# Four pieces of work moved inside the attention steps of a fused attention and Fourier-mix kernel

## The chip, the cores and the metric

One core of a Trainium2 chip runs the whole program in one launch. The metric is the device time of a launch in microseconds (us), lower is better. The engines of a core are TensorE (PE for its matmuls, PEld for its weight loads), VectorE (DVE), ScalarE (ACT), GpSimd (POOL) and SyncE (SP). In this program SP computes nothing: nearly all DMAs are issued from its queue, in the order in which the program wrote them, and an issue that has to wait for data holds up every issue behind it.

## What is computed

For 8 batches of 8 heads, with 576 rows and a head size of 64, an attention with a threshold; its result, laid out as 576 x 512 per batch, goes through a two-dimensional Fourier transform of which the real part is added, a layer norm, and a channel MLP of 512 to 2048 to 512. All is in fp32.

```python
scores = scale * np.matmul(q, k.transpose(0, 1, 3, 2))
thresh = np.max(scores, axis=-1, keepdims=True) - tau
scores = np.where(scores >= thresh, scores, -1000000000.0)
attn = np.exp(scores - max); attn = attn / (sum + 1e-09)
x = (attn @ v)                       # (B,H,S,D) -> (B, S, H*D)
u = x + np.real(np.fft.fft(np.fft.fft(x, axis=1), axis=2))
un = (u - mean) / np.sqrt(var + 1e-06)
out = u + np.maximum(un @ w_ch1, 0.0) @ w_ch2
```

## The kernel before

**Steps.** Two heads make a pair `n`, four pairs make a batch, and a pair takes five steps `t` = 0 to 4 of 128 query rows each (the fifth has the last 64 rows of both heads). So there are 160 steps `i`, 20 in a batch; below, s is `i` modulo 20, so that s = 0 to 4 belong to a batch's first pair, 5 to 9 to its second, and so on. The pairs of a batch are taken in the order 1, 3, 0, 2 of the heads' pairs; the first two of these have v stored with its columns reversed, and need their rows 0 and 64 exchanged afterwards.

**A step of the main loop (lines 1764 to 1837, batches 2 to 7).** TensorE makes the scores (`scores`). DVE takes the row maxima (line 518), ACT the exponentials (524), DVE compares and sums (539), and ACT scales by the sums (552). Around this the loop calls `fill` three times. A `fill` issues a little of the MLP of earlier rows: as much as a running budget says, so it is the same number of pieces in every run. The call order in a step is: scores; the values of an earlier pair; `softmax_first`; `fetch`; `fill(True)`; `softmax_second`; `blocks`; row exchanges that stand in `swaps`; `weights_in_parts`; `fill`; `softmax_third`; `prep_pair` and the like; `fill`; loads of v, q or k.

**The MLP** of 512 rows (`two_level`) runs a first layer of 28 blocks of 8 matmuls each (line 1288, about 10 steps), and then a second of 49 blocks of 4 matmuls (line 1437, the other 10 steps). Its weights come by DMA into a ring of five places (`ensure`, lines 1155 to 1165), four places ahead. A block of the first layer with m = 7 adds onto the bank that the block with m = 6 left, so it can start only when DVE has added that bank to `hs` (line 1225). Between them lies one other block.

**Two ways to transpose the softmax's result** for the product with v. In the second layer TensorE transposes and ACT copies. In the first layer (`phase[0] == 1`) a step goes by DMA (`decide`): `blocks` lets DVE sort its tile into blocks of 32 x 32 (line 601, into the one room `et_room`) and SP write it to memory (602), one step after the step itself; `fetch` reads it back in four DMAs two steps after (611). `et_room` can be written again when the DMA of 602 has landed. From batch 3 on these are, in each batch, the steps s = 6, 7, 8 (second pair), 10 to 13 (third pair) and 15 (fourth pair), 40 in all.

**The product with v** (`values_in_parts`) has a first part of 256 query columns, and a second of 320. By default the first part is issued at t = 3 and the second at t = 1 of the next pair. Where the pair went by DMA, the first part is issued at t = 0 of the next pair, and the second at t = 1 of the next pair behind `fill(True)` (`late_values`). So these second parts are at s = 11 and s = 16.

**Row exchange.** `swap_rows` copies two rows out by two DMAs (line 759) and back crosswise by two more (763). For a batch's first pair it is called in `fold_rows`: copy of the tile on POOL (line 779), both pairs of DMAs, and then the fold itself (792 onward). `fold_more` takes the next piece of it: at t > 2 and from some blocks of the MLP. The first piece falls to the last `fill` of s = 6.

**prep_pair** (403 to 416) lets DVE transpose k and q of the next pair (lines 410, 411, 413) at t = 3. **v_of** (578) lets POOL make the reversed v, called in `weights_in_parts` at t = 1. **load_raw** loads q at the end of t = 0 and k at the end of t = 1; **load_v** loads v at the end of t = 2.

Of the kernel before, what the change touches and what calls it, by code (L numbers as in the profile page):

```python
# [47 lines left out]
def kernel(  # L48
# [500 lines left out]
    def softmax_third(i):  # L549
        nh, e, den = steps[i]  # L550
        for j in range(nh):
            nc.scalar.activation(  # L552
                out=e[:, S * j : S * (j + 1)], in_=e[:, S * j : S * (j + 1)], func=ACT.Copy,
                scale=den[:, j : j + 1],
            )
        if nh == 1:
            nc.scalar.copy(e[:, S : S + 64], e[:, 512:S])
        steps[i] = (e, None)
# [4 lines left out]
    def in_blocks(n):  # L563

        return n >= 3 * NPAIR
# [5 lines left out]
    def decide(i):  # L571

        n, t = divmod(i, NT)
        by_dma[i] = i < B * NPAIR * NT and in_blocks(n) and t < 4 and (
            phase[0] == 1 or t == 2 and by_dma[i - 1]
        )

    def v_of(n):

        src = heads[n][2]  # L580
        if PAIRS[n % NPAIR] % 2 == 0:
            return src
        vt = sb.tile([128, 10, D], FP32, tag="vr", bufs=1, name="v_rev")
        nc.gpsimd.tensor_copy(vt[:, :, 0:1], src[:, :, 0:1])
        last = src[:, :, D - 1 : D]
        down = bass.AP(
            tensor=last.tensor, offset=last.offset,
            ap=[list(last.ap[0]), list(last.ap[1]), [-1, D - 1]],
        )
        nc.gpsimd.tensor_copy(vt[:, :, 1:D], down)  # L590
        return vt
# [3 lines left out]
    def blocks(i):  # L595

        if not by_dma[i]:
            return
        e = steps.pop(i)[0]
        out_ = et_room.rearrange("p (b c q) -> p c b q", b=4, c=NC9)  # L600
        nc.vector.transpose(out_, e[:, 0 : 2 * S])
        nc.sync.dma_start(out=scratch[i % 3][:, :], in_=et_room)

    def fetch(i):

# [16 lines left out]
    def weights_in_parts(i):  # L622

        n, t = divmod(i, NT)
        if in_blocks(n) and t == 0:
            heads[n] = (*heads[n][0:2], v_of(n), None, None)
        if by_dma.get(i):
            return
        e, rec = steps.pop(i)
        if in_blocks(n) and t < 4:  # L630
            to = by_block[:, first_block(t) : first_block(t) + 4]
            pe = ps.tile([128, 4, 128], FP32, tag="mm", bufs=4, name="pe")
            nc.tensor.transpose(pe[:, 0, :], e[:, 512:640], ident[:, :])
            nc.scalar.copy(to[:, :, 4, :], pe[:, 0, :].rearrange("p (a q) -> p a q", q=32))  # L634
            for j in range(2):
                pw = ps.tile([128, 4, 128], FP32, tag="mm", bufs=4, name="pw")
                if j == 1:
                    yield
                for c in range(4):
                    c0 = (S + D) * j + 128 * c  # L640
                    nc.tensor.transpose(pw[:, c, :], e[:, c0 : c0 + 128], ident[:, :])  # L641
                nc.scalar.copy(
                    to[:, :, 5 * j : 5 * j + 4, :],
                    pw[:, :, :].rearrange("p c (a q) -> p a c q", q=32),
                )
            return
        if in_blocks(n):
            pe = ps.tile([128, 4, 128], FP32, tag="mm", bufs=4, name="pe")
            nc.tensor.transpose(pe[:, 0, :], e[:, 512:640], ident[:, :])
            for j in range(2):  # L650
                hp = slice(64 * j, 64 * j + 64)
                nc.scalar.copy(
                    by_block[hp, 2:4, 4, :],
                    pe[hp, 0, hp].rearrange("p (a q) -> p a q", q=32),
                )
            pw = ps.tile([128, 4, 128], FP32, tag="mm", bufs=4, name="pw")
            for c in range(4):
                nc.tensor.transpose(pw[:, c, :], e[:, 128 * c : 128 * c + 128], ident[:, :])
            for j in range(2):
                for a in range(2):  # L660
                    nc.scalar.copy(
                        by_block[:, 2 + a, 5 * j : 5 * j + 4, :],
                        pw[:, :, 64 * j + 32 * a : 64 * j + 32 * a + 32],
                    )
            return
        if t in (0, 2):

            e_t, ends = early_e_t, early_ends  # L670
            vt = v_of(n) if t == 0 else heads[n][2]
            heads[n] = (*heads[n][0:2], vt, e_t, ends)
        e_t, ends = heads[n][3:5]
        q0 = 128 * (t - (0 if t < 2 else 2))
        pe = ps.tile([128, 4, 128], FP32, tag="mm", bufs=4, name="pe")
        nc.tensor.transpose(pe[:, 0, :], e[:, 512:640], ident[:, :])
        kept = 1
        if rec is not None:
            nc.tensor.transpose(pe[:, 1, :], rec, ident[:, :])
            kept = 2  # L680
        if t < 4:
            nc.scalar.copy(ends[:, 0:kept, q0 : q0 + 128], pe[:, 0:kept, :])
        else:
            for j in range(2):
                hp = slice(64 * j, 64 * j + 64)
                nc.scalar.copy(ends[hp, 0:kept, q0 : q0 + 64], pe[hp, 0:kept, hp])
        qs = slice(q0, q0 + (128 if t < 4 else 64))
        for j in range(2 if t < 4 else 1):
            pw = ps.tile([128, 4, 128], FP32, tag="mm", bufs=4, name="pw")
            if j == 1:  # L690
                yield
            for c in range(4):
                c0 = (S + D) * j + 128 * c
                nc.tensor.transpose(pw[:, c, :], e[:, c0 : c0 + 128], ident[:, :])  # L694
            if t < 4:
                nc.scalar.copy(e_t[:, 4 * j : 4 * j + 4, qs], pw[:, :, :])
            else:
                nc.scalar.copy(
                    e_t[:, :, qs].rearrange("p (j c) q -> p j c q", j=2),
                    pw[:, :, :].rearrange("p c (j q) -> p j c q", j=2),  # L700
                )
# [50 lines left out]
    def swap_rows(n, later=False):  # L752
        b, p = n // NPAIR, PAIRS[n % NPAIR]
        x = xs[b][p]
        if p % 2:

            swap = sb.tile([2, S], FP32, tag="half", bufs=1, name="swap")
            for j in range(2):
                nc.sync.dma_start(out=swap[j : j + 1, :], in_=x[64 * j : 64 * j + 1, :])

            def back():
                for j in range(2):
                    nc.sync.dma_start(out=x[64 * j : 64 * j + 1, :], in_=swap[1 - j : 2 - j, :])

            if late and later:
                swaps.append(back)
            else:
                back()

# [4 lines left out]
    def fold_rows(n):  # L774
        b, p = n // NPAIR, PAIRS[n % NPAIR]
        if late and n % NPAIR == 0:
            assert not mixes
            x = sb.tile([128, S], FP32, tag=f"x{p}", bufs=1, name=f"x{p}")
            nc.gpsimd.tensor_copy(x[:, :], xs[b][p][:, :])
            xs[b][p] = x  # L780
            swap_rows(n)
            yield
        x = xs[b][p]

        half = sb.tile([128, 2, HALF], FP32, tag="half", bufs=1, name="half")
# [874 lines left out]
    def fold_more():  # L1660
        if folds and next(folds[0], True):
            folds.pop(0)
# [101 lines left out]
    for i in range(2 * per_batch, total + 3):  # L1764
# [3 lines left out]
        values = iter(())  # L1768
        if i < total:
            scores(i)  # L1770
        late_values = None
        if t == 3 and i < total and not by_dma.get(i - 2):
            values = values_in_parts(n, 0)
        elif t == 0 and by_dma.get(i - 4):
            values = values_in_parts(n - 1, 0)
        elif t == 1 and n > 0:
            while folds:
                fold_more()
            values = values_in_parts(n - 1, 1)
            if by_dma.get(i - 3):  # L1780
                values, late_values = iter(()), values
        next(values, None)
        if i < total:
            softmax_first(i)
# [7 lines left out]
                pass  # L1792
            start_batch(i // per_batch - 1)
        fill(True)
        for _ in late_values or ():
            pass
        if i < total:
            softmax_second(i)
        while held:
# [4 lines left out]
            swaps.pop(0)()  # L1804
        if mixes:
            mix(1)
        if t == 1:
            if n % NPAIR:
                folds.append(fold_rows(n - 1))
            else:  # L1810
                last_fold = fold_rows(n - 1)
                next(last_fold)
        weights = weights_in_parts(i - 1) if i <= total else iter(())
# [6 lines left out]
        next(weights, None)  # L1820
        if i < total:
            softmax_third(i)
            if t == 1:
                prep_ends(n)
            if t == 2 and n + 1 < B * NPAIR:
                scale_q(n + 1)
            if t == 3 and n + 1 < B * NPAIR:
                prep_pair(n + 1)
        if wanted:
            wanted.pop().factors()  # L1830
        if i % per_batch == 1:
            next(last_fold)
        fill()
        if t == 2 and n + 1 < B * NPAIR:
            load_v(n + 1)
        if t < 2 and n + 1 < B * NPAIR and len(loaded.get(n + 1, ())) == t:
# [51 lines left out]
```

## Time and profile before

| what | value |
|---|---|
| median of 3 runs | 1634.24 us (1628.0 to 1637.57) |
| profiled execution, its own time | 1636.11 us |
| its span, first to last instruction | 1634.0 us |
| busy: PE, DVE, ACT, POOL | 93%, 69%, 55%, 50% |
| granted TensorE clock, mean | 0.973 |
| DMA engines, by SP's queue | 60.6% of the span |
| DVE transposes of line 601 | 40, 1366 ns each |
| DVE transposes of lines 410, 411, 413 | 32 each, 761, 242 and 778 ns |
| DMAs of line 602: issue to landing | 40, median 4.1 us |
| DMAs of line 611: issue to landing | 160, median 3.9 us |
| DMAs of 759 and 763: issue to landing | 32 each, 1.8 and 1.7 us |

A line of the waits names who waited, for whom, then microseconds in total, times, and the longest. A line of the timeline gives start, duration, engine, line, operation and the tiles written and read; in brackets is the engine's idle time before it and what ended it. A line of the windows gives a stretch's length, the busy time of each engine, the granted TensorE clock, and the share of the DMA engines.

### The profile page before, as it was taken

What the parts mean: (1) busy time and instruction counts of PE and PEld (TensorE: products, weight loads), DVE (VectorE), ACT (ScalarE), POOL (GpSimd) and SP (SyncE); (2) the same over time, 40 slices, a digit from 0 to 9 for tenths busy, and PEclk for the clock granted to TensorE, in tenths of its full rate; (3) what the DMA queues carried; (4) which work ended last, traced back from release to release, by engine and by line L of the source; (5) the groups of instructions that cost most, each with busy time, mean ns of one, the idle gap of its engine ahead of it and who ended that gap; (6) DMA issues with size and microseconds to landing.
All of it is one profiled execution on the core that took longest, in us unless ns stands there. A gap on an engine that the chain in (4) does not pass through costs nothing.

```text
span 1634.0 us, 27080 instructions
## 1 busy us (share of the span) xinstructions
PE 1523.9 (93%) x9410; PEld 1166.9 (71%) x9410; DVE 1130.0 (69%) x2137; ACT 904.9 (55%) x1913; POOL 813.3 (50%) x1002
## 2 busy tenths in 40 slices
PE   8998989999999989998999899998999899999997
PEld 4555545556787867876787677776787678889987
DVE  7997786846769567766677577856677666636537
ACT  5775565545666556655666566665566566233231
POOL 6784663034454623536253724553264625547646
PEclk9999999999999999999999999999999999999998
DMA  7423221645945389737975588628974696556755
GB/s 159 125 56 113 74 74 36 190 144 177 285 149 165 94 253 261 203 97 203 248 203 143 141 252 244 187 79 230 255 205 127 178 264 203 186 160 230 238 188 191
DMA packets 296253, 286.26 MB, mean 175 GB/s; under 512 B 202643, under 2 KB 241045, under 8 KB 295222
## 3 DMA queue, kind: packets, MB, share of 16 engines
q1 hardware_dynamic: 293606, 284.23, 60.6%
q8 instruction: 76, 1.25, 0.3%
q10 hardware_dynamic: 2512, 0.30, 0.2%
q14 instruction: 59, 0.48, 0.1%
HBM read 231.10 MB, written 53.22 MB: 174 GB/s over the span
## 4 chain that ended last, share of the span: by engine, by line
PE 60%; DVE 19%; DMA 6%; ACT 6%; issue 4%; POOL 2%; SPq 2%; DVEq 0%; ACTq 0%; POOLq 0%
PE ph L1288 16%; PE po L1437 15%; PE pv L730 8%; PE sc L439 6%; PE po L1015 4%; PE ph L991 2%; DMA v_in<-in_v_dram 2%; PE pw L641 2%; DVE e L479 2%; PE py L864 2%; DMA w<-f 2%; PE pw L694 2%; ACT e L524 1%; DVE e L539 1%; DVE neg L518 1%
## 5 line engine op out<-in xcount | busy, mean ns | idle before, releaser
L518 DVE TENSOR_REDUCE neg<-sc 128x1 f32<-128x576 f32 x216 | 153.8, 749 | 127.0 <-PE sc L439 117.0
L524 ACT ACTIVATE e<-sc,neg 128x576 f32<-128x576 f32 x216 | 158.4, 733 | 136.5 <-DVE neg L518 135.8
L1437 PE MATMUL po<-w,w_all 128*128 128x128 f32 x1792 | 229.6, 278 | 1.2 <-ACT et_all L634 0.8
L1437 PEld LDWEIGHTS po<-w,w_all 128*128 128x128 f32 x1792 | 214.6, 193 | 11.0 <-issue 6.2
L1234 POOL TENSOR_TENSOR w<-hs 128x512 f32<-128x512 f32 x32 | 42.1, 1318 | 352.0 <-ACT hs L1230 325.3
L539 DVE SCALAR_TENSOR_TENSOR e<-sc,thr,e 128x576 f32<-128x576 f32 x216 | 168.4, 813 | 47.4 <-ACT thr L528 47.4
L1288 PE MATMUL ph<-w_all,w 128*128 128x256 f32 x672 | 168.9, 401 | 33.4 <-DVE hs L1225 33.4
L1288 PE MATMUL ph<-u_t,w 128*128 128x256 f32 x768 | 183.1, 383 | 0.0
L439 PE MATMUL sc<-kT,qT 64*128 64x288 f32 x1024 | 171.2, 434 | 9.4 <-DVE e L479 8.1
L1288 PEld LDWEIGHTS ph<-w_all,w 128*128 128x128 f32 x672 | 130.9, 199 | 65.1 <-POOL w_all L1337 23.6
L552 ACT ACTIVATE e<-e,den 128x576 f32<-128x576 f32 x216 | 156.8, 770 | 25.3 <-DVE den L546 24.9
L1288 PEld LDWEIGHTS ph<-u_t,w 128*128 128x128 f32 x768 | 142.3, 190 | 29.9 <-issue 9.0
L439 PEld LDWEIGHTS sc<-kT,qT 64*128 64x128 f32 x1024 | 94.2, 187 | 64.3 <-issue 35.7
L1230 ACT ACTIVATE hs<-hs 128x512 f32<-128x512 f32 x64 | 54.0, 843 | 152.6 <-DVE hs L1225 152.6
L1337 POOL TENSOR_TENSOR w_all<-w_all 128x128 f32<-128x128 f32 (+2 forms) x160 | 119.6, 765 | 33.0 <-DVE w_all L1455 22.4
L1437 PE MATMUL po<-w,hs 128*128 128x128 f32 x960 | 126.3, 279 | 0.0
L1437 PEld LDWEIGHTS po<-w,hs 128*128 128x128 f32 x960 | 117.3, 194 | 9.1 <-issue 7.7
L1225 DVE TENSOR_TENSOR hs<-ph,hs 128x512 f32<-128x512 f32 x64 | 60.5, 945 | 84.1 <-PE ph L1288 78.8
L730 PE MATMUL pv<-et_all,v_rev 128*64 128x256 f32 (+1 forms) x640 | 86.2, 416 | 4.3 <-DMA out_dram<-u 2.6
L730 PE MATMUL pv<-et_all,v_in 128*64 128x256 f32 (+1 forms) x640 | 86.4, 414 | 3.9 <-ACT e L524 1.6
L906 POOL TENSOR_TENSOR u_t<-x,tmp 128x289 f32<-128x289 f32 (+1 forms) x45 | 34.0, 756 | 105.3 <-DVE tmp L901 105.3
L471 ACT ACTIVATE e<-sc,neg 128x576 f32<-128x576 f32 x72 | 52.8, 733 | 45.3 <-DVE neg L463 45.2
(235 smaller groups left out, 3204.3 us busy)
## 6 DMA issues: line engine op xcount, KB each, us to landing
w<-f SPq DMA_DIRECT2D x304, 512.0 KB, 4.4
e_blocks<-w SPq DMA_DIRECT2D x40, 576.0 KB, 4.1
et_all<-e_blocks SPq DMA_DIRECT2D x160, 144.0 KB, 3.9
hs<-in_moe_w_ch_dram SPq DMA_DIRECT2D x23, 512.0 KB, 4.7
q_in<-in_q_dram SPq DMA_DIRECT2D x128, 72.0 KB, 4.3
out_dram<-u SPq DMA_DIRECT2D x36, 256.0 KB, 4.2
k_in<-in_k_dram SPq DMA_DIRECT2D x124, 72.0 KB, 3.9
v_in<-in_v_dram SPq DMA_DIRECT2D x64, 128.0 KB, 4.7
```

Source lines behind the costliest of these rows:

```text
L439: nc.tensor.matmul(sc[j][:, c, 0:HALF], qT[hp, 128 * t : 128 * t + 128], kT[hp, k0 + HALF * c : k0 + HALF * (c + 1)], start=True, stop=True,)
L518: nc.vector.tensor_reduce(out=neg[:, j : j + 1], in_=sc[j][:, :, 0:HALF], axis=AXIS_XY, op=ALU.max, negate=True,)
L524: nc.scalar.activation(out=ej, in_=sc[j][:, :, 0:HALF], func=ACT.Exp, bias=neg[:, j : j + 1], scale=1.0)
L539: nc.vector.scalar_tensor_tensor(out=ej, in0=sc[j][:, :, 0:HALF], scalar=thr[:, j : j + 1], in1=ej, op0=ALU.is_ge, op1=ALU.mult, accum_out ...
L552: nc.scalar.activation(out=e[:, S * j : S * (j + 1)], in_=e[:, S * j : S * (j + 1)], func=ACT.Copy, scale=den[:, j : j + 1],)
L730: nc.tensor.matmul(pv[64 * j : 64 * j + 64, 0:m], vt[:, 2 * c + j, :], right, start=(c == 0), stop=(c == 4), skip_group_check=True,)
L1015: nc.tensor.matmul(po[:, :], hs[:, BT * j + 128 * t : BT * j + 128 * (t + 1)], w2[j], start=(j == 0), stop=(j == NJ - 1),)
L1225: nc.vector.tensor_tensor(out=to, in0=bank, in1=to if other is None else other, op=ALU.add)
L1230: nc.scalar.activation(out=to, in_=to, func=ACT.Relu)
L1288: nc.tensor.matmul(bank[:, 256 * q : 256 * q + 256].rearrange("p (two n) -> p two n", two=2), left[:, 256 * c + 128 * q : 256 * c + 128 * ...
L1337: return lambda: eng.tensor_tensor(out=to, in0=to, in1=other, op=ALU.add)
L1437: nc.tensor.matmul(to, lefts[m][j][:, s], right_[:, 128 * s : 128 * (s + 1)], start=fresh and s == 0, stop=s == 3, skip_group_check=True,)
```

## The change

Five edits, all in the order of work:

1. The row exchange of a batch's first pair, in `fold_rows`, is given out in three pieces: copy; DMAs out; DMAs back. Before they were one piece.
2. The DMA that writes a sorted tile leaves `blocks` for a function of its own, `keep_blocks`, called at the step's end behind the last `fill`, and before the loads of v, q and k.
3. `prep_pair` is called behind the last `fill` and not ahead of it.
4. The second part of the values, for pairs that went by DMA, is issued at t = 2 of the next pair, right behind the scores, and not at t = 1 behind the first `fill`. With it the pair's fold is put on the list a step later, and `v_of` moves from t = 1 to t = 2.
5. `decide` takes a step t = 0 by DMA too where the last whole step of the pair before went by DMA.

```diff
@@ decide
         by_dma[i] = i < B * NPAIR * NT and in_blocks(n) and t < 4 and (
-            phase[0] == 1 or t == 2 and by_dma[i - 1]
+            phase[0] == 1 or t == 2 and by_dma[i - 1] or t == 0 and by_dma[i - 2]
         )
@@ blocks
         nc.vector.transpose(out_, e[:, 0 : 2 * S])
-        nc.sync.dma_start(out=scratch[i % 3][:, :], in_=et_room)
+
+    def keep_blocks(i):
+
+        if by_dma.get(i):
+            nc.sync.dma_start(out=scratch[i % 3][:, :], in_=et_room)
@@ weights_in_parts
-        if in_blocks(n) and t == 0:
-            heads[n] = (*heads[n][0:2], v_of(n), None, None)
@@ swap_rows
             if late and later:
                 swaps.append(back)
+            elif late:
+                return back
             else:
                 back()
@@ fold_rows
             xs[b][p] = x
-            swap_rows(n)
             yield
+            back = swap_rows(n)
+            yield
+            if back:
+                back()
+                yield
@@ main loop
-        late_values = None
...
         elif t == 1 and n > 0:
             while folds:
                 fold_more()
+            if not by_dma.get(i - 3):
+                values = values_in_parts(n - 1, 1)
+        elif t == 2 and by_dma.get(i - 4):
             values = values_in_parts(n - 1, 1)
-            if by_dma.get(i - 3):
-                values, late_values = iter(()), values
...
         fill(True)
-        for _ in late_values or ():
-            pass
+        if t == 2 and i < total and in_blocks(n):
+            heads[n] = (*heads[n][0:2], v_of(n), None, None)
...
-        if t == 1:
+        if t == (2 if by_dma.get(NT * n - 2) else 1):
             if n % NPAIR:
                 folds.append(fold_rows(n - 1))
...
-            if t == 3 and n + 1 < B * NPAIR:
-                prep_pair(n + 1)
         if wanted:
             wanted.pop().factors()
         if i % per_batch == 1:
             next(last_fold)
         fill()
+        keep_blocks(i - 1)
+        if t == 3 and n + 1 < B * NPAIR:
+            prep_pair(n + 1)
         if t == 2 and n + 1 < B * NPAIR:
             load_v(n + 1)
```

## The prediction

> **What bounds the kernel.** I read the page first, then the waits, then the time order of one batch. The page says that PE is the bound on the average, and that its clock was not always whole.
>
> ```profile
> PE 1523.9 (93%) x9410; PEld 1166.9 (71%) x9410; DVE 1130.0 (69%) x2137; ACT 904.9 (55%) x1913; POOL 813.3 (50%) x1002
> ```
>
> The waits, of PE, of DVE and of SP's queue, say what PE's pauses are made of.
>
> ```profile
> PE ph L1288 <- DVE hs L1225: 34.7, 14, 5.1
> DVE w L601 <- DMA e_blocks<-w: 27.8, 12, 5.5
> SPq L759 <- POOL x L779: 27.7, 5, 5.5
> SPq L763 <- DMA swap<-x: 19.1, 16, 2.3
> SPq L602 <- DVE w L601: 68.2, 20, 6.6
> SPq L611 <- DMA e_blocks<-w: 11.8, 11, 1.9
> ```
>
> PE's largest wait is for DVE's add of line 1225. DVE waited for the sorted tile's room, and SP waited five times, once in each batch from 3 to 7, for the copy of line 779. The timeline shows that these are one event.
>
> ```profile
> 562.45 1.17 SPq L759 DMA_DIRECT2D swap<-x  x2
> 564.81 1.19 SPq L763 DMA_DIRECT2D x<-swap  x2
> 566.05 2.19 SPq L140 DMA_DIRECT2D k_in<-in_k_dram  x4
> 568.83 0.43 SPq L602 DMA_DIRECT2D e_blocks<-w  x1
> 574.96 1.38 DVE L601 STREAM_TRANSPOSE w<-e 128x1152 f32<-128x1152 f32 x1 [5.27 <-DMA e_blocks<-w]
> 576.26 0.73 DVE L410 STREAM_TRANSPOSE kT<-k_in 128x576 f32<-128x576 f32 x1
> 577.29 0.78 DVE L413 STREAM_TRANSPOSE qT<-q_in 128x576 f32<-128x576 f32 x1
> 577.99 0.65 DVE L1225 TENSOR_TENSOR hs<-ph,hs 128x512 f32<-128x512 f32 x1
> 578.79 3.75 PE L1288 MATMUL ph<-w_all,w 128*128 128x256 f32 x8 [4.89 <-DVE hs L1225]
> ```
>
> SP stood at the exchange until POOL's copy was done (562.4), then for the landing, then issued k, and only at 568.83 the tile sorted at 563.25. The next sort waited 5.27 us for its landing, k and q stood between it and the add, and PE stood for 4.89 us. Afterwards PE ran slowly; the windows have the length, five engines' busy time, the clock, and the DMA share:
>
> ```profile
> 577.90:584.70 6.80, 5.91 (x14) 4.78 (x15) 5.28 (x10) 2.17 (x5) 0.66 (x1) 0.50 0.92 319
> 603.10:609.60 6.50, 6.50 (x33) 5.16 (x32) 4.70 (x8) 4.61 (x8) 0.79 (x1) 1.00 0.91 222
> 616.10:624.30 8.20, 6.50 (x29) 5.04 (x27) 7.06 (x13) 3.47 (x6) 0.70 (x1) 1.00 1.05 307
> ```
>
> The first is half clock in s = 9. The second is a step of 6.5 us with no pause (s = 12). The third is s = 14, with PE idle 1.70 us: there DVE's chain was 601, 410, 411, 413 and then 1225 (619.95), with no DMA late.
>
> From the starts of the score matmuls I took each step's length in batches 3 to 7:
>
> - s = 9: 14.3, 9.5, 13.7, 13.6, 13.0 (PE idle 4.9, 3.0, 4.6, 4.1, 5.0 of it)
> - s = 14: 8.2, 10.2, 8.2, 11.0, 8.2 (idle 1.7 to 2.9)
> - s = 11 and 12 together: 14.8, 17.5, 14.5, 15.0, 14.7; s = 10: 9.4, 11.3, 9.4, 9.4, 9.4
> - s = 16 and 17 together: 16.1 to 16.3; s = 18: 11.1, 12.1, 10.7, 10.4, 10.4
>
> **What the Trainium skill says.** "TensorE: Matmul & The Clock Gate", Part 1: the PE clock is at half after an idle window of about 3.4 us, in windows that run freely. The trace agrees: half-clock windows of 3.41 or 6.83 us follow four of the five pauses at s = 9 and two at s = 14, with matmuls 0.43 us apart and not 0.215. So a pause costs more than itself. The table that opens the page says that VectorE's queue is strictly first in, first out; the trace agrees (1225 stands behind 601). "DMA: Bandwidth & Descriptors", Anatomy of one DMA: a DMA's semaphore wait happens on the issuing sequencer; SP at 562.45 shows it. The same page, Two DMAs through the same engine are not ordered: a DMA that reads what another wrote must wait for its completion before it is issued. So each fetch waits on SP for its tile's landing (11 short waits, 11.8 us in all).
>
> **The change, part by part.**
>
> *Edit 5* changes nothing. The first layer runs from t = 1 of the second pair to t = 0 of the fourth in every batch, since the budget is the same; no pair's t = 3 goes by DMA with the next t = 0 outside the first layer. It stays 40 steps.
>
> *Edits 1 and 2, at s = 6 to 9.* The copy stays at the end of s = 6, but the DMAs out come with the first layer's third block, at the end of s = 7. SP is free for k at about 557 and reaches the exchange at about 562.6 (the weight load ahead of it waits for the block before), when the copy is done. The tile, sorted by 564.6, is written at about 564.7, four microseconds earlier, and lands 4.1 to 5 later, by 569.7. The next sort is ready at 569.7 (564.58, when the scores began, plus the 5.1 that scores, maximum, exponential, compare and sum took). It waits 0 to 1 us, and not 5.27.
>
> *Edit 3.* The add then follows the sort: 569.7 + 1.37 + 0.65 = 571.7, or 572.7 with the wait. PE needs it at 573.9. Pause: none. The 1.75 us of k and q (0.76 + 0.24 + 0.78) go behind the add, ahead of the next maximum, where they already stood before. At s = 14 the add comes 1.75 us sooner too, against a pause of 1.70.
>
> Bare work of s = 9 and 14: scores (4 x 0.243) and three blocks of eight matmuls at 0.215, with 0.3 of issue, is 6.4; s = 12 measured 6.5. The five steps s = 9 sum to 64.1, less 5 x 6.5 = 31.6 to gain; s = 14: 45.8 - 32.5 = 13.3. What is late next: at s = 9 the tile of s = 7 is written at about 572.9 and lands near 578, while the sort behind it is ready at 576.4; DVE stands 1.5 us with no matmul behind it. At s = 14 the compare of line 539 must free the score banks: it ended at 623.07, and the scores would want them at 622.6. So I take 5.3 a batch at s = 9, and 2.2 at s = 14: **26.5 + 11 = 37.5 us**.
>
> *Edit 2 elsewhere.* In s = 11 to 14 DVE ends its sort near the step's end anyway (610.22 + 1.36 = 611.6 for scores at 603.1), and SP issued at 611.61: the write can hardly come later. Its landing (4.1 to 6.6 by the trace) is due 5.1 us into the next step. DVE may stand up to 1.5 us; the add that follows has 2.3 us in hand (PE needs it 6.5 + 2.96 after the step's start, it is done at 7.1). Bounds: 0 to +5 us over all; I take 0. The fetch waits on SP up to 4 us a time. Behind it stand weight loads, four places or eight blocks ahead, at 2.8 blocks a step: hidden. A fetched tile is used two steps later or more, but for s = 15: fetched in s = 17, used in s = 18; there edit 4 makes s = 17 longer, and covers it.
>
> *Edit 4.* The second part (20 matmuls, 2.84 us) leaves s = 11 and 16 for s = 12 and 17: no sum of PE changes. At s = 11 it no longer waits for its tiles (idle 0.26 to 1.30) and s = 10 and 11 of batch 4, both behind SP's jam, lose 1.9 and 2.5. I take **5 us** over the five batches (0 to 8). At s = 16 block (3, 7) is left right behind (3, 6), with DVE's add between: matmuls end at 3.0, add 0.65 with its latencies by 3.9: 0.9 us each, **-4.5**; s = 18's waits, 2.5 in all, go: sum **-2** (-5 to +2). The fold a step later and v_of a step later are POOL's (50% busy), with needs two steps away or more, except the reversed v of the first pair, needed half a step after; POOL idles 1.7 us there. 0.
>
> **Sum:** 37.5 + 5 - 2 = 40.5. The profiled execution took 1636.1: 1595.6. It lies 1.9 above the median of the runs, which is inside their spread, so I do not shift by it. Forecast **1595 us**.
>
> **Rivals.**
>
> *The jam only moves (1618).* For: the DMA engines are at 0.97 to 1.05 of full in s = 9 and in s = 13 and 14, so landings of 6 us may stay, and shorter steps raise the share (0.77 of 97 us is 0.85 of 88). Against: in s = 7 and 8 they were at 0.25 and 0.52, so there is room to spread. Then s = 9 gains half (13), s = 14 its 1.70 five times less one bank wait (7), edit 4 loses 2: 1636 - 18 = 1618.
>
> *No change (1633).* The gain is eaten by DVE, whose 7.06 us of 8.2 in s = 14 makes it the bound. Against: it is 4.7 of 6.5 in s = 12.
>
> *Slower (1655): the sorted tile's room is freed too late.* One mechanism, at line 601 in every step by DMA: the write is issued at the step's end behind weight loads that wait for PE, and its landing ends the next sort's wait. It decides from a landing 7.4 us after the step's end (5.1, when the sort is due, plus the 2.3 in hand). If it took 9 us (SP behind its own fetch waits), the add would be 1.6 late at s = 9, 12 and 14 in five batches, and each pause long enough to halve the clock would add 1.7: 15 x 3.3 = 50, less what edits 1 and 3 still gain (30): 1636 + 20. For: SP's queue has 68 us of waits for the sort and 11.8 for the write. Against: the slowest landing in the trace was 6.6.
>
> **How the numbers follow.** Forecast 0.66 (1580 to 1612), jam moves 0.16, no change 0.07, slower 0.11. 0.5% is 8 us, about what a measurement of this kernel can tell from no change. Faster: 0.66 + 0.16 = 0.82; same 0.07; slower 0.11. The upper end must take in the second case with some room, 1622; the lower end is all gains whole (31.6 + 13.3 + 8 + 2 = 55), 1580: 1580 to 1622.
>
> **What would show it.** Right: SP's wait for line 779 is gone; line 601 waits less than 12 us in all, and PE for 1225 less than 12; no half clock at s = 9 and 14, which last 6.5 to 7.5 us; PE at s = 16 waits about 0.9 for line 1225. Wrong: line 601 waiting in s = 11 to 14, weight loads among PE's releasers, or line 602 landing 7 us and more after issue. The forecast is wrong if PE still stands at s = 9, or if the time saved there comes back as waits of the scores for line 539.

## The result, and the profile after

The changed kernel took 1648.83 us, median of 7 runs (1645.69 to 1658.43), beside 1632.84 us for the kernel before (7 runs, 1628.0 to 1637.57). The ratio is 1.0106, with a 95% interval of 1.0077 to 1.0135. It is slower by about 1%; 1595 us was forecast. The profiled execution took 1648.8 us and its span 1647.0, which is 12.9 us more than before.

In the changed kernel a few lines have other numbers: the add of 1225 is now 1233, the first layer's matmul 1296, ACT's relu 1238, the write of the sorted tile 606, the fetch 615, the exchange 761 and 765. Line 601 has kept its number. In the variants below the same lines stand a few numbers higher or lower.

The page's busy times after:

```profile
PE 1529.5 (93%) x9410; PEld 1167.9 (71%) x9410; DVE 1125.3 (68%) x2137; ACT 904.2 (55%) x1913; POOL 818.3 (50%) x1002
```

DVE, ACT and POOL do what they did, and PE is 5.6 us longer with the same number of matmuls. So the loss is in pauses and in half clock, not in work: over batches 3 to 7, where a batch's steps go by DMA, PE idled for 66.8 us and not 60.2, and was busy for 836.3 and not 828.3, of which 55.8 at half clock and not 45.9. The waits of SP's queue after, in us, times and longest:

```profile
SPq L606 <- DVE w L601: 67.7, 26, 7.2
...
SPq L615 <- DMA e_blocks<-w: 28.7, 24, 4.0
...
SPq L765 <- DMA swap<-x: 10.3, 6, 3.1
```

And those of the engines:

```profile
DVE w L601 <- DMA e_blocks<-w: 35.2, 16, 3.9
...
PE pw L660 <- ACT x L741: 19.2, 10, 2.5
...
PE ph L1296 <- DVE hs L1233: 16.3, 15, 2.5
...
PE pe L651 <- ACT e L557: 11.1, 8, 3.3
```

SP's wait for POOL's copy (27.7 us before) is gone, and PE's wait for the add has fallen from 34.7 to 16.3. But DVE waits longer for the sorted tile's room than before (35.2 against 27.8, in 16 waits and not 12), and two waits of PE have come up: for ACT's copy of a bank of the values (2.8 before, in 4 waits), and for ACT's part of the softmax of a pair's last step.

Where the time went shows best in the length of each step, taken from the starts of the score matmuls and summed over batches 3 to 7 (s = 19 over 3 to 6). The last three columns are experiments told of below; all columns come from one profiled execution each. That of the kernel without edit 2 was the fastest of its five, 4 us under their median.

| s | before | after | after, without edit 2 | edit 1 alone | edit 2 alone |
|---|---|---|---|---|---|
| 9 | 64.1 | 32.0 | 32.0 | 31.6 | 73.9 |
| 10 | 48.9 | 67.8 | 53.1 | 52.1 | 52.1 |
| 11 and 12 | 76.8 | 72.8 | 72.8 | 74.9 | 73.1 |
| 14 | 45.9 | 44.5 | 34.1 | 46.3 | 74.5 |
| 15 | 48.9 | 76.7 | 66.9 | 50.1 | 51.9 |
| 16 and 17 | 80.3 | 84.6 | 84.6 | 80.3 | 80.0 |
| 18 | 54.7 | 51.8 | 53.5 | 55.0 | 64.2 |
| 19 | 30.0 | 33.8 | 33.8 | 30.0 | 30.0 |
| all steps of these batches | 888.5 | 903.1 | 868.2 | 859.5 | 938.4 |

The changed kernel gains 32.1 us at s = 9, more than was forecast there. It loses 18.9 at s = 10 and 27.8 at s = 15, the steps right behind those in which time was to be gained.

The timeline of batch 3 after, from the exchange on:

```profile
562.18 1.17 SPq L761 DMA_DIRECT2D swap<-x  x2
...
562.30 1.36 DVE L601 STREAM_TRANSPOSE w<-e 128x1152 f32<-128x1152 f32 x1
...
563.68 0.33 SPq L606 DMA_DIRECT2D e_blocks<-w  x1
...
569.54 1.38 DVE L601 STREAM_TRANSPOSE w<-e 128x1152 f32<-128x1152 f32 x1 [0.77 <-DMA e_blocks<-w]
569.58 1.75 SPq L615 DMA_DIRECT2D et_all<-e_blocks  x4
...
571.38 1.43 SPq L765 DMA_DIRECT2D x<-swap  x2
...
572.91 0.52 SPq L1169 DMA_DIRECT2D w<-f  x1
...
573.53 0.38 SPq L606 DMA_DIRECT2D e_blocks<-w  x1
...
578.78 1.38 DVE L601 STREAM_TRANSPOSE w<-e 128x1152 f32<-128x1152 f32 x1 [2.70 <-DMA e_blocks<-w]
...
580.09 1.19 DVE L1233 TENSOR_TENSOR hs<-ph,hs 128x1024 f32<-128x1024 f32 x1
...
581.37 1.06 ACT L1238 ACTIVATE hs<-hs 128x1024 f32<-128x1024 f32 x1 [6.05 <-DVE hs L1233]
...
582.33 0.76 ACT L552 ACTIVATE e<-e,den 128x576 f32<-128x576 f32 x1
...
583.42 0.33 PE L651 MATMUL pe<-ident,e 128*128 128x128 f32 x1 [1.89 <-ACT e L557]
583.75 0.74 ACT L524 ACTIVATE e<-sc,neg 128x576 f32<-128x576 f32 x1
...
584.57 0.74 ACT L524 ACTIVATE e<-sc,neg 128x576 f32<-128x576 f32 x1
...
585.19 0.38 ACT L741 COPY x<-pv 128x256 f32<-128x256 f32 x1
...
585.62 1.11 PE L660 MATMUL pw<-ident,e 128*128 128x128 f32 x4 [1.88 <-ACT x L741]
```

The first three lines are close to the forecast: SP is at the exchange at 562.18, and writes the tile 0.02 us behind its sort. The tile of the next step is the loser. Its sort ends at 570.92, but from 569.58 on SP issues one DMA after the other: the fetch (1.75), the exchange back (1.43), a weight load (0.52). The write goes out 2.61 us behind the sort and lands 5.24 later, 9.2 us after the step's end (569.60, where the next scores begin with their weight loads). The sort of 578.78 has stood 2.70 us for it. Behind that sort stands DVE's add, behind the add ACT's relu, and in ACT's order behind the relu the scaling (552, 557) of the pair's last step. PE transposes that step's tile early in s = 10 and waits 1.89 us. Then the two exponentials of the new step, pushed back by the same pause, stand in ACT's order ahead of the copy of line 741, and PE waits another 1.88 us for this copy before the last transposes.

The chain of waits in this stretch, with start and duration, has the same links in a row (four of them shown):

```profile
573.53 5.24 DMA e_blocks<-w
...
581.37 1.06 ACT hs L1238
...
585.31 0.27 ACT x L741
...
585.62 1.11 PE pw L660 x4
```

What the pause does to the clock, in three windows of about 3.41 us at s = 10 and three at s = 14 (length, busy time of PE, PEld, DVE, ACT and POOL, clock, DMA share, GB/s):

```profile
581.00:584.41 3.41, 0.85 (x4) 0.26 (x2) 2.98 (x6) 3.01 (x6) 3.41 (x7) 1.00 1.00 297
584.41:587.82 3.41, 2.19 (x8) 1.93 (x9) 3.04 (x9) 3.34 (x12) 0.46 (x3) 0.50 1.07 227
587.82:591.24 3.42, 3.42 (x10) 2.70 (x9) 0.03 (x1) 1.08 (x3) 0.00 (x0) 0.50 0.99 292
...
615.14:618.55 3.41, 1.27 (x6) 0.81 (x5) 2.48 (x3) 0.57 (x2) 3.25 (x5) 1.00 0.54 141
618.55:621.96 3.41, 3.41 (x10) 2.70 (x9) 2.37 (x5) 1.54 (x4) 0.17 (x1) 0.50 0.97 237
621.96:625.30 3.34, 3.34 (x23) 2.18 (x24) 0.90 (x5) 0.00 (x0) 0.00 (x0) 1.00 1.01 413
```

A window in which PE was busy for 0.85 us of 3.41 is followed by two at half clock. So s = 10 took 16.4 us here, with only 3.8 us of idle PE in it; before it took 9.4.

### The profile page after: what moved, and what is told of

The parts are those of the page before. It is cut to its first block, busy times and chain, and to the rows that moved or that the text cites. A ratio compares the mean times of both kernels' runs of the same rounds, so it can differ in the third digit from the quotient of the medians.

```text
span 1647.0 us, 27082 instructions
## 1 busy us (share of the span) xinstructions
PE 1529.5 (93%) x9410; PEld 1167.9 (71%) x9410; DVE 1125.3 (68%) x2137; ACT 904.2 (55%) x1913; POOL 818.3 (50%) x1002
## 4 chain that ended last, share of the span: by engine, by line
PE 56%; DVE 19%; ACT 8%; DMA 8%; issue 4%; POOL 3%; SPq 2%; DVEq 0%; ACTq 0%; POOLq 0%
PE po L1445 15%; PE ph L1296 13%; PE pv L732 7%; DMA e_blocks<-w 7%; PE sc L439 6%; PE po L1023 3%; PE ph L999 2%; PE pw L643 2%; ACT e L524 2%; PE py L872 2%; DVE e L479 2%; PE pw L696 1%; DVE neg L518 1%; DVE e L539 1%; DVE hs L1233 1%
## 5 line engine op out<-in xcount | busy, mean ns | idle before, releaser
L524 ACT ACTIVATE e<-sc,neg 128x576 f32<-128x576 f32 x216 | 158.6, 734 | 158.9 <-DVE neg L518 158.8
L1242 POOL TENSOR_TENSOR w<-hs 128x512 f32<-128x512 f32 x32 | 44.5, 1392 | 312.3 <-ACT hs L1238 312.3
L1296 PE MATMUL ph<-u_t,w 128*128 128x256 f32 x768 | 194.6, 401 | 0.0
L1296 PE MATMUL ph<-w_all,w 128*128 128x256 f32 x672 | 162.2, 389 | 15.1 <-DVE hs L1233 15.1
L1296 PEld LDWEIGHTS ph<-u_t,w 128*128 128x128 f32 x768 | 150.6, 201 | 32.9 <-issue 9.0
L1233 DVE TENSOR_TENSOR hs<-ph,hs 128x512 f32<-128x512 f32 x64 | 60.2, 941 | 87.8 <-PE ph L1296 82.5
L601 DVE STREAM_TRANSPOSE w<-e 128x1152 f32<-128x1152 f32 x40 | 54.6, 1366 | 35.2 <-DMA e_blocks<-w 35.2
```

Of the source, the lines that this page charges most:

```text
L524: nc.scalar.activation(out=ej, in_=sc[j][:, :, 0:HALF], func=ACT.Exp, bias=neg[:, j : j + 1], scale=1.0)
L1233: nc.vector.tensor_tensor(out=to, in0=bank, in1=to if other is None else other, op=ALU.add)
L1296: nc.tensor.matmul(bank[:, 256 * q : 256 * q + 256].rearrange("p (two n) -> p two n", two=2), left[:, 256 * c + 128 * q : 256 * c + 128 * ...
```

## The experiments

These theories were set against each other. **A**: the write at the step's end (edit 2) goes out behind the step's weight loads and lands late; DVE stands at line 601, ACT and PE behind it. **B**: edit 4 crowds DMA and DVE at s = 12. **C**: edit 3 puts the last step's maximum behind k and q, so the softmax is late for PE's transposes. **D**: edit 3 only moves the pause from s = 14 to s = 15. **E**: edit 3 brings its price, and a loss comes from edit 4. The kernel before took 1634.41, 1633.84 and 1633.19 us in the three groups of runs. Ratios are to it, with 95% intervals.

### Without edit 2

```diff
         nc.vector.transpose(out_, e[:, 0 : 2 * S])
+        nc.sync.dma_start(out=scratch[i % 3][:, :], in_=et_room)
...
-        keep_blocks(i - 1)
```

> The changed kernel with edit 2 undone: the sorted tile is written right behind its sort. Theory A (the write stands behind the step's weight loads, lands late, DVE stands at line 601 and ACT and PE behind it at the two steps that follow a pair's last step): DVE waits under 10 us at line 601, steps s = 10 and 15 are back at 9.4 to 10.5 us, s = 14 is 6.5 to 7.5, and the time is about 1600 us, 2% under the kernel before. Theory B (edit 4 crowds the DMA engines and DVE around s = 12, so that landings are long whatever the write's place): line 601 still waits over 20 us, and the time stays at 1640 to 1650.

Measured: 1619.07 us, ratio 0.9917 (0.989 to 0.9944). The waits of this kernel:

```profile
PE pw L656 <- ACT x L737: 14.4, 10, 1.9
...
DVE w L601 <- DMA e_blocks<-w: 10.5, 12, 1.9
...
PE ph L1292 <- DVE hs L1229: 9.7, 12, 1.4
```

The waits at line 601 fall from 35.2 to 10.5 us, near what A expected, and the kernel is now faster than before; B expected 1640 us or more. In the table, s = 10 loses 14.7 us of its length, s = 14 10.4 and s = 15 9.8: 34.9 of 903.1. So edit 2 is what makes the change slower. It isn't all that is wrong with it: A expected about 1600 us, and s = 15 at 9.4 to 10.5 us, where it takes 12.7 to 14.2 (66.9 in all, against 48.9 before).

### Edit 2 alone, on the kernel before

```diff
-        nc.sync.dma_start(out=scratch[i % 3][:, :], in_=et_room)
+    def keep_blocks(i):
+        if by_dma.get(i):
+            nc.sync.dma_start(out=scratch[i % 3][:, :], in_=et_room)
...
         fill()
+        keep_blocks(i - 1)
```

> The kernel before with edit 2 alone. Theory A: slower than before, about 1650 us or more, with longer waits at line 601 in steps s = 8, 9, 13 and 14. Theory B: as before, 1628 to 1638.

Measured: 1683.74 us, ratio 1.0302 (1.0283 to 1.032).

```profile
DVE w L601 <- DMA e_blocks<-w: 81.6, 21, 7.7
...
PE ph L1292 <- DVE hs L1229: 58.5, 13, 7.3
```

Moving one DMA costs 49 us, as A expected and B did not. With k and q still ahead of the add, most of DVE's wait reaches PE (58.5 of 81.6 us): s = 14 goes from 45.9 to 74.5 us, s = 9 from 64.1 to 73.9.

### Without edit 4, and without edit 3

The first puts the second part of the values, the fold and `v_of` back where they were; the second puts `prep_pair` back ahead of the last `fill`.

```diff
...
-        elif t == 2 and by_dma.get(i - 4):
             values = values_in_parts(n - 1, 1)
+            if by_dma.get(i - 3):
+                values, late_values = iter(()), values
...
```

> The changed kernel with edit 4 undone: the second part of the values is at s = 11 and 16 again. Theory A: still slower than before, 1640 to 1650 us, with s = 10 and 15 at 11 us and more. Theory B: under 1620 us, and line 601 waits under 12 us.

```diff
+            if t == 3 and n + 1 < B * NPAIR:
+                prep_pair(n + 1)
...
         fill()
         keep_blocks(i - 1)
-        if t == 3 and n + 1 < B * NPAIR:
-            prep_pair(n + 1)
```

> The changed kernel with edit 3 undone: k and q are transposed ahead of the last stretch again. Theory A: the late landing still decides and the add of line 1233 is 1.75 us later still, so 1650 to 1665 us. Theory C (edit 3 puts the last step's maximum behind k and q, and so makes its softmax late for TensorE's transposes at s = 10 and 15): 1635 us or less, and s = 10 and 15 at 9.4 to 10.5 us.

Measured: without edit 4 1663.84 us, 1.0178 (1.0135 to 1.0222); without edit 3 1632.45 us, 0.9991 (0.9974 to 1.0009). Neither time is what A expected (1640 to 1650, and 1650 to 1665). B, which expected under 1620 us without edit 4, falls: beside edit 2, edit 4 helps by some 12 us (0.0072 of 1634; the two intervals touch). With it s = 12 is 9.4 us long and not 6.5, which leaves the writes of s = 11 to 13 more time; without it s = 14 took 63.7 us against 44.5, and the sort of s = 13 waited 2.9 to 4.7 us in every batch against 0.9 to 3.0. At s = 18 PE waited 8.9 us for fetched tiles, and the step took 62.5 us against 51.8. Edit 3, which was to gain, costs 19 us among the others (0.0115 of 1634), so A had its sign wrong, and E falls where it says that edit 3 brings its price. The time without edit 3 is in C's range (1635 or less), but the steps aren't: s = 10 took 10.8 to 13.3 us and s = 15 9.8 to 14.0, where C had 9.4 to 10.5.

### Edit 1 alone

```diff
+            elif late:
+                return back
...
-            swap_rows(n)
             yield
+            back = swap_rows(n)
+            yield
+            if back:
+                back()
+                yield
```

> The kernel before with edit 1 alone. My sum gave edits 1 and 2 together the whole pause at s = 9. If edit 1 alone frees SP, s = 9 falls from 12.8 us on the mean to 7 to 9, k and q still ahead of the add: 1605 to 1620 us. If the jam is the write's place in the queue behind k's loads, s = 9 stays over 11 us and the time over 1627.

Measured: 1603.28 us, ratio 0.9819 (0.9794 to 0.9843). It has these waits:

```profile
PE ph L1294 <- DVE hs L1231: 13.4, 9, 3.0
...
PE pw L658 <- ACT x L739: 6.3, 7, 1.5
...
DVE w L601 <- DMA e_blocks<-w: 5.1, 5, 1.3
```

The gain at s = 9 is edit 1's (32.5 us in the table), and edit 2 adds nothing to it. It is more than was expected of it: s = 9 took 6.2 to 6.6 us, not 7 to 9.

### Edits 1 and 4; and q, k prepared a step later still

```diff
         if i < total:
             softmax_first(i)
+        if t == 4 and n + 1 < B * NPAIR:
+            prep_pair(n + 1)
```

The first kernel has edits 1 and 4 (and edit 5, which changes no step). The second is the first with this piece, in place of the call at t = 3: k and q then stand behind the maximum of the last step, and no longer ahead of it.

> Edits 1 and 4 alone (the write right behind its sort, k and q ahead of the last stretch). Theory D (edit 3 only moves the pause of s = 14 to s = 15 and adds a little at s = 19, because the last step's softmax on DVE and ACT is the chain that binds there): s = 14 at 8 to 9 us, s = 15 at 10, s = 19 at 7.8, and 1605 to 1615 us, faster than the run with edits 1, 3 and 4 (1619). Theory E (edit 3 gains what it was priced at, 1.7 to 2.2 us a batch, and what is lost at s = 15 comes from edit 4): 1625 to 1635 us.

> Edits 1 and 4, with k and q transposed one step later still, behind the row maximum of the pair's last step (t = 4), where DVE waits for ACT's exponential. Theory D: the last step's maximum comes 1.75 us sooner, so s = 14 stays at 6.2 to 7 us and s = 15 falls to 10 to 11.5: 1595 to 1607 us. Theory E: as with edits 1, 3 and 4, 1615 to 1625, since s = 15 keeps its 13 us.

Measured: 1608.3 us, 0.9848 (0.9821 to 0.9876), and 1617.72 us, 0.9901 (0.9879 to 0.9924). Beside edit 1, edit 4 brings nothing; its interval overlaps that of edit 1 alone (0.0029 between the ratios is 5 us). The first time is in D's range and not in E's. The second is not in D's (1595 to 1607) but in E's: s = 15 takes 12.5 to 14.7 us, 69.3 in all, and the kernel is 9 us slower than without the piece. Its trace shows that the piece did what it was to do, and that another wait took its place. In batch 3 the last step's maximum started 2.39 us behind the first scores of s = 14 and not 3.91, but the next sort then stood 2.58 us for the room, and line 601 waited 19.2 us in all, against 8.8 without the piece. So this run decides nothing between C, D and E: the one room comes first.

### All five edits, with two rooms for the sorted tile

```diff
-    et_room = w1[2][:, HID // 2 : HID // 2 + 4 * 9 * 32]
+    et_rooms = [w1[2][:, 1152 * u : 1152 * (u + 1)] for u in range(2)]
...
-            nc.sync.dma_start(out=scratch[i % 3][:, :], in_=et_room)
+            nc.sync.dma_start(out=scratch[i % 3][:, :], in_=et_rooms[i % 2])
...
-        room = n % 5
+        room = n % 4
...
-            ensure(n + 4 if g > 1 or second else min(n + 4, 13 if index < 24 else 15))
+            ensure(n + 3 if g > 1 or second else min(n + 3, 13 if index < 24 else 15))
```

The second room is paid for by one place of the weight ring.

> The changed kernel, all its edits, with two rooms for the sorted tile in turn; the place comes from the weights' ring, which has four places instead of five. Theory A (the room freed late is what edit 2 costs): line 601 waits under 5 us in all, s = 10 and 14 fall to about 10 and 6.5, and the time is at most 1620 us. If what edit 2 costs is SP's queue instead (fetches that wait for the landing, weights behind them): the time stays at 1640 us or more, with weight loads among PE's releasers.

Measured: 1606.67 us, ratio 0.9839 (0.9819 to 0.9859). The waits:

```profile
PE ph L1296 <- DVE hs L1233: 7.7, 10, 0.9
...
PE pw L660 <- ACT x L741: 4.8, 7, 1.1
...
PE pv L732 <- DMA et_all<-e_blocks: 4.5, 3, 2.5
...
PE po L1445 <- DMA w<-f: 1.9, 3, 0.8
...
PE pv L732 <- DMA w<-f: 1.8, 1, 1.8
```

Line 601 waits nowhere, though the writes still land late: 6.5 to 9.3 us after issue in s = 13 and 14. The time and the steps are what A expected (at most 1620 us; s = 10 took 9.4 to 10.3 us, s = 14 6.2 to 6.3). So a late write costs little in itself: PE waited 4.5 us for fetched tiles. What costs is that the one room comes free late. The ring of four places shows in the last two lines, 3.7 us of waits of PE for weights.

### Edit 3 alone; edits 1 and 3; edits 1 and 3 with two rooms

```diff
-            if t == 3 and n + 1 < B * NPAIR:
-                prep_pair(n + 1)
...
         fill()
+        if t == 3 and n + 1 < B * NPAIR:
+            prep_pair(n + 1)
```

> The kernel before with edit 3 alone (k and q behind the last stretch). My sum gave it 2.2 us a batch at s = 14 and part of s = 9: 1615 to 1625 us. Theory D (the pause of s = 14 only moves, and may halve the clock where it lands): s = 14 at 6.2 to 7, s = 15 at 11 to 14 instead of 10, and 1630 to 1645 us.

> Edits 1 and 3. With edit 1 alone it was 1603. Theory D: 1605 to 1620, s = 14 short and s = 15 long. If edit 3 gains its price: 1590 to 1597.

> Edits 1 and 3 with two rooms for the sorted tile (the weights' ring has four places), the write right behind its sort. With the room no longer waited for, DVE reaches the last step's maximum sooner, and edit 3 should gain: s = 14 at 6.3, s = 15 at 10 to 11.5, 1590 to 1600 us. If ACT and the bank behind the values bind s = 15 whatever the room, it stays at 1603 to 1612.

Measured: 1632.78 us, 0.9996 (0.9985 to 1.0008); 1609.04 us, 0.9849 (0.9824 to 0.9874); 1604.96 us, 0.982 (0.9801 to 0.984). (The second and third kernel have edit 5 too.) Edit 3 alone moves the time and brings nothing: s = 14 falls from 45.9 to 34.0 us, s = 15 rises from 48.9 to 59.1, s = 9 falls from 64.1 to 52.7 and s = 10 rises from 48.9 to 58.5. Its waits name what is late next:

```profile
PE pw L658 <- ACT x L739: 13.1, 9, 1.9
```

That wait was 2.8 us before. The copy itself comes no later than it did. Batch 3 from the first scores of s = 14 on, in the kernel before:

```profile
616.09 1.13 PE L445 MATMUL sc<-kT,q_ends 128*128 128x288 f32 x4
...
620.52 0.74 DVE L518 TENSOR_REDUCE neg<-sc 128x1 f32<-128x576 f32 x1
...
629.77 0.38 ACT L739 COPY x<-pv 128x256 f32<-128x256 f32 x1
...
630.20 0.66 PE L658 MATMUL pw<-ident,e 128*128 128x128 f32 x4 [0.31 <-ACT x L739]
```

And with edit 3 alone:

```profile
614.23 1.13 PE L445 MATMUL sc<-kT,q_ends 128*128 128x288 f32 x4
...
618.67 0.72 DVE L518 TENSOR_REDUCE neg<-sc 128x1 f32<-128x576 f32 x1
...
627.89 0.38 ACT L739 COPY x<-pv 128x256 f32<-128x256 f32 x1
...
628.33 0.65 PE L658 MATMUL pw<-ident,e 128*128 128x128 f32 x4 [1.42 <-ACT x L739]
```

The last step's maximum starts 4.43 and 4.44 us behind these scores, and the copy 13.68 and 13.66; in no batch does the copy's place differ by more than 0.1 us. K and q stood ahead of this maximum in the kernel before too, so C falls by its premise. The chain of DVE and ACT through s = 14 and 15 is as long as it was. PE reaches its end sooner, and waits there. With two rooms s = 15 still takes 58.3 us. So D holds: the pause is at the copy of line 739, also where the room is free.

Edits 3 and 4 do more harm together than apart. With edit 1, each of them costs 5 us, which is within the noise (1609.04 and 1608.3 beside 1603.28 us). With edit 1 and both, the kernel took 1619.07 us (the run without edit 2), and its interval lies apart from these. There line 601 waits 10.5 us and s = 15 takes 66.9; with edits 1 and 3 it is 4.0 and 61.3. With two rooms all five edits are as fast as edits 1 and 3 (1606.67 and 1604.96), which fits the room as the reason; no run shows it apart.

### Edit 1, with the copy of the bank ahead of the exponentials

```diff
         next(values, None)
+        if t == 0 and by_dma.get(i - 4):
+            next(values, None)
         if i < total:
             softmax_first(i)
```

> Edit 1, and ACT copies the values' bank at s = 10 and 15 ahead of that step's exponentials and not behind them. If TensorE's transposes there wait for that copy because of its place in ACT's order: the waits of up to 1.5 us at s = 10 and 15 go, 1595 to 1602 us. If the exponentials are then late for DVE: 1603 to 1610.

Measured: 1599.13 us, ratio 0.9779 (0.9747 to 0.981). Its profiled execution took 1591.45 us, the fastest of its four; the other three took 1598.95 to 1602.73. The timeline at s = 10:

```profile
577.71 0.38 ACT L739 COPY x<-pv 128x256 f32<-128x256 f32 x1
577.98 0.76 ACT L524 ACTIVATE e<-sc,neg 128x576 f32<-128x576 f32 x1
...
579.40 0.60 PE L658 MATMUL pw<-ident,e 128*128 128x128 f32 x4
```

The copy now comes ahead of the exponentials, and PE doesn't wait for it there: line 658 has no wait for line 739 left. s = 10 takes 9.4 us in all five batches, and s = 15 9.4 to 9.7. So with edit 1 the copy's place in ACT's order was the link that passed a late step on to PE. Whether edit 3 keeps its 11.9 us of s = 14 with the copy in this place was not tried. This is the fastest version tried, and faster than both kernels of the case. Against edit 1 alone the intervals overlap (0.9794 to 0.9843 there), so what the copy adds to it isn't settled.

## Why the prediction was wrong

In a row, from runs in three groups: the kernel before took 1634 us, edit 1 alone 1603, with edit 3 1609, with edit 4 as well 1619, with edit 2 as well 1649. The prediction's largest gain came true. Two of its terms failed: edit 2 outside s = 6 to 9, put at nothing, and edit 3, put at a gain of 11 us.

**Edits 1 and 2 at s = 6 to 9: right in time, wrong in whose gain it is.** Forecast 26.5 us, with the tile written at once and a sort that waits 0 to 1 us; the step was 6.2 us in four batches and 7.0 in one (bare work was put at 6.4), the sort waited 0.77 us in batch 3 and in no other, and the gain was 32.1. Edit 1 alone gives all of it. The two edits were priced as one, and so edit 2 was never asked what it does by itself.

**Edit 2 elsewhere: this step failed.** The text has "the write can hardly come later", bounds 0 to +5 us, and takes 0. Undoing it gains 0.0189 of the time, 31 us. Two things in the step were wrong. First, the room does come free later. Without edit 2, and with it, where the trace tells the landing:

| tile written in | issue behind the sort's end, without | with | landing behind the issue, without | with |
|---|---|---|---|---|
| s = 8 | 0.6 to 1.6 us | 1.3 to 2.6 | 3.9 to 4.4 us | 5.2 to 5.3 |
| s = 12 | 0.03 to 0.6 | 0.03 to 0.7 | 5.0 to 6.1 | 6.2 to 7.1 |
| s = 13 | 1.3 to 2.2 | 0.9 to 1.0 | 3.8 to 4.9 | 6.5 to 8.1 |

The issue, about which the step argued, is the smaller part (at s = 13 it even comes earlier). The landing, which it took from the trace of the kernel before, is the larger: 1 to 3 us. In each of these steps, in every batch, the write with edit 2 has one more weight load of 512 KB close ahead of it. The order among the DMAs is what the edit changes; that the queue itself does this was not measured apart. Second, "DVE stands 1.5 us with no matmul behind it" at s = 9 was wrong by its second half: DVE stood 1.2 to 3.1 us, and the matmuls behind it are two engines away, through the add, the relu, the scaling and the transposes of the next step. I followed the queue behind the waiting sort to the end of DVE's own, and not on into ACT's. The Trainium skill, "Perfetto Trace Analysis", Tensor Engine Instruction, says that the execution queue of ACT too is strictly first in, first out; the trace agrees, since ACT's scaling of 582.33 started only at the end of the relu of 581.37, although its own input had been ready since 576.08.

**Edit 3: the direct gain was right, its sum wrong; this step failed too.** Forecast 2.2 us a batch at s = 14, 11 in all; alone it gains 11.9 there. The question "what is late next" was answered with the compare of line 539. It was ACT's copy of line 741 at s = 15 and 10, at the end of a chain through DVE and ACT that edit 3 doesn't shorten: the maximum and the copy keep their places behind the start of s = 14. The two steps together took 94.8 us before and 93.1 with edit 3 alone. What s = 14 gains, s = 15 gives back, with 3.8 us more at s = 19, where the sum had nothing.

**Edit 4: right in its own steps, not in the sum.** Forecast +5 at s = 11 and 12, -4.5 at s = 16, +2.5 at s = 18; measured +4.0 (1.9 of it already with edit 1 alone), -4.3 (s = 16 and 17; PE idle 0.85 us in each s = 16, against 0.9) and +2.9. That it helps the writes of s = 11 to 13 beside edit 2 wasn't seen, nor that it costs 10 us beside edits 1 and 3. **Edit 5** changed nothing: line 601 still has 40 instructions.

**The clock.** Half-clock windows did follow the pauses. Before, four stretches began at s = 9 and two at s = 14; after, three at s = 10, two at s = 14 and five at s = 15. In batches 3 to 7 half clock rose from 51.2 to 61.4 us. The mean clock hides it (0.974, and 0.973 before), since elsewhere it fell. The prediction took the two at s = 14 as agreeing with an idle window; PE was busy there for 1.42 and 0.56 us of the 3.41 ahead.

**The rivals.** The slower one named the right place (line 601), nearly the right cause (a write behind weight loads; but of the 15 loads next ahead of the writes of s = 8, 12 and 13, one alone waited for PE), and nearly the time: 1655 against 1648.8. The time is in part luck: it put 50 us of loss on the late room, where edit 2 brought 30 and edits 3 and 4 the other 16. It put the landing at 9 us after the step's end; the trace has 9.2 for the tile written behind s = 8 and 9.4 behind s = 12 of batch 3 (scores at 606.62, landed by 616.05). It was given 0.11 by a false comparison. Its threshold of 7.4 us counts from the step's end, but the argument against it, "the slowest landing in the trace was 6.6", counts from the issue, and is that of a fetch; the slowest write of line 602 took 6.4. Between the two lie the rest of DVE's chain, the sort and SP's issues, 3.9 us at s = 8 (569.60 to 573.53). In the kernel before, the write of s = 12 went out at 611.61, 2.0 us after that step's end by the prediction's own numbers (603.1 + 6.5); with a landing of 6.4 that is 8.4, beyond the threshold. Where the rival went wrong: it had the adds late at s = 9, 12 and 14, with PE waiting for them; at s = 9 PE waited a step later, through ACT, s = 12 was spared, and s = 15 was hit.

## What to carry to other kernels

- Price each edit by itself before pricing two together, and build the one-edit kernel first: here one piece of five held the gain (-30 us), another held a loss of 31 to 49.
- A DMA that frees the only room of its kind belongs right behind the work that fills the room. Moving it to a "quiet" point costs all that the queue issues in between, and its landing counts from the same origin as the need.
- Where an in-order engine waits, follow the queue behind it, then the queues of those who wait for that, until PE or nothing is reached. When a pause leaves one step, look for the next step's first wait on ACT, not only for the same wait's rest.

## What the runs showed of the hardware

- In these traces the clock changes only after whole windows of 3.41 us, and it fell without an unbroken pause of a whole window. In the window before 618.55 PE was busy for 1.27 us of 3.41, its longest pause was 2.14 us, and the next window ran at half clock. The Trainium skill, "TensorE: Matmul & The Clock Gate", Part 1, speaks of an idle window of about 3.4 us; here 37% busy counted as one. A window at half clock in which PE was busy for 2.19 of 3.41 us was followed by another at half clock, so the way back asks for more. In the profiled executions of all 14 kernels, every full-clock window in which PE was busy for less than 1.40 us was followed by half clock, and none with more than 2.23; in between both occurred. No half-clock window with less than 2.80 us was followed by full clock.
- The same 576 KB write at s = 13 landed in 3.8 to 4.9 us, or in 6.5 to 8.1, ahead of its step's first weight load or 0.47 us behind it. In batch 3 the DMA engines were as full in the first case (1.04, 612.10 to 617.01) as in the second (0.99, 618.45 to 624.96).
